# Strassen's scheme for the first feed-forward product of the last two token blocks of a fused attention and two-layer kernel

## The chip, the cores and the metric

The kernel runs on one core of one Trainium2 chip. The metric is the device time of one execution in microseconds (us), smaller is better. The engines of the core are named as in the profile: PE (TensorE, matrix products), PEld (its weight loads, which overlap PE), DVE (VectorE), ACT (ScalarE), POOL (GpSimd) and SP (SyncE, which here only issues DMA transfers).

## The reference

Three stages follow one another. The second and third are what the change touches.

```
x = causal attention with decay (4 batches x 8 heads, 576 positions, 64 wide)   # 2304 tokens x 512
h = x @ w_in                                  # 2304 x 512 @ 512 x 2048
g = maximum(0.01 * h, h)
y = g @ w_out                                 # 2304 x 2048 @ 2048 x 512
h2 = y @ w_in2                                # 2304 x 512 @ 512 x 1024
solu = h2 * softmax(h2)
ln = (solu - mean) / sqrt(var + 1e-6) * g_ln
out = ln @ w_out2                             # 2304 x 1024 @ 1024 x 512
```

All inputs and the output are float32.

## The kernel before

**Numbers.** Every operand of a large product is held as two fp16 halves, a high part and a low part (the rounding rest). One product of a 128x128 piece of weights with a row of tokens is therefore three matmuls: high by high, high by low, low by high. Making the halves takes two instructions for each tile: a copy to fp16 (`copy_f`, any of ACT, DVE, POOL) and a subtraction of that copy from the float32 tile (`sub_f`, DVE or POOL).

**Blocks.** The 2304 tokens are 9 blocks of 256, taken in the order 0, 1, 4, 5, 3, 2, 8, 6, 7. The first feed-forward product of a block is done for 8 pairs of 128-wide pieces of w_in, `k` = 0 to 7, in two groups `g` of four pairs. `hidden` does it for one block and one `k`: 24 matmuls of 256 columns into one PSUM bank `ps_f` (three such banks), then ACT applies leaky relu twice (once into the fp16 tile, once in place), and DVE subtracts the two for the low half. After four `hidden` follows the second product of that block and group, 4 pieces of 24 matmuls of 256 columns.

**Second layer.** `layer2` does a block of the third product (y by w_in2) by Strassen's scheme already: 7 products of 6 matmuls of 512 columns, into banks `ps_g` and halves of the two large PSUM tiles `ph`, with DVE forming the sums out of PSUM (`plus`, `full`). Softmax and normalization follow on ACT, DVE and POOL, then transposes by DMA into `tr`, and the output product, 18 times 24 matmuls of 512 columns. The weights w_in2 and w_out2 are loaded, joined (`whole`), bounded (`bound`, `sums`) and split into halves (`split_w2i`, `load_w2o`, `split_w2o`) ahead of that, beside the feed-forward products.

**Order.** Every instruction is first recorded as an op of a plan, with an engine (or several that may take it), an estimated duration, a priority, the tiles that it reads and writes, and ops that it must follow. A list scheduler in the kernel then turns the plan into one fixed order for each engine; it also gives each op that has several engines to one of them, with the weights `WEIGHT` and `WEIGHT2` on DVE's cost. Tiles belong to tags (`wz`, `y2`, `tr`, `hl2`, `g`, ...) with a fixed number of places; `heirs` passes places that are free for good on to other tags. So a change of priorities, of weights or of tags moves instructions in places far from it. DMA transfers are issued by SP in its own order.

Of the kernel before, what the change touches and what calls it, by code (L numbers as in the profile page):

```python
# [7 lines left out]
F32 = mybir.dt.float32  # L8
# [33 lines left out]
AV = -2.05  # L42
EP = 1307.15
LD = 10.04
# [14 lines left out]
NYO = 2  # L59
NWY = 14  # L60
NY2 = 2
NHL2 = 2
NTR = 3
PWL = 500.0
DMAR = 320.0
YB_ENGS = ("DVE",)
VB_ENGS = ("DVE",)
# [9 lines left out]
US0 = 21.76  # L77
HST = 2.56
TB = 256
# [43 lines left out]
WEIGHT = {"DVE": 7.06}  # L123
WEIGHT2 = {"DVE": 1.06}
HEAT = 0.25
# [280 lines left out]
def body(tc, kqa, kq, vt, f, wa, w2i, w2o, gln, out):  # L406
# [511 lines left out]
    def load_wi(k, prio):  # L918
# [102 lines left out]

    def ffn(blk, g, prio):
        eprio = prio - EP
        first, last = blk not in YO, LEFT.setdefault(blk, 2) == 1
        LEFT[blk] -= 1
# [3 lines left out]
        if first:  # L1029
            YO[blk], YPD[blk] = [P.buf("yo") for q in range(2)], []  # L1030
        gs = {k: hidden(k, XB[blk], prio + HST * i, eprio + i) for i, k in enumerate(GRP[g])}
        for q in range(2):
            ps, yo = P.buf("ps_f"), YO[blk][q]
            for d in range(2):

                def pe(d=d, q=q, ps=ps):
                    for k in GRP[g]:
                        for i in range(2):
                            y_mms(ps.t[:, TB * d:TB * d + TB], 2 * k + i, 2 * q + d, gs[k], k == GRP[g][0] and i == 0, k == GRP[g][-1] and i == 1)

                P.op(PE, 6 * len(GRP[g]) * mmr(TB), pe, prio + YD + 4 * q + 2 * d, r=list(gs.values()) + [WO[2 * k + i] for k in GRP[g] for i in range(2)],
                     **({"w": [ps]} if d == 0 else {"rw": [ps]}))
# [14 lines left out]
    def load_y(blk, prio):  # L1057
        yw, sy, y = P.buf("yw"), P.buf("sy"), P.buf("y2")
        for q in range(2):
# [14 lines left out]
        sub_f(X(2), A(1, 0), X(1), 256, prio, S_ENGS, w=[(sy, 2)], r=[yw, (sy, 1)])  # L1074
        pieces = [(512 * e, 512, lambda e=e: four(yw.t[:, 0:1024])[:, e::2], (yw, "e%d" % e)) for e in range(2)] + [(1024, 768, lambda: four(sy.t), sy)]
        for at, n, v, k in pieces:
            copy_f(lambda at=at, n=n: four(y.t[:, 0, at:at + n]), v, n, prio, scale=lambda: ev(IY + blk), w=[(y, (0, at))], r=[k, (EX, ("iy", blk))])
        for at, n, v, k in pieces:
            sub_f(lambda at=at, n=n: four(y.t[:, 1, at:at + n]), v, lambda at=at, n=n: four(y.t[:, 0, at:at + n]), n, prio, scale=lambda: ev(IY + blk),
                  w=[(y, (1, at))], rw=[k], r=[(y, (0, at)), (EX, ("iy", blk))])  # L1080
        return y

    def layer2(tb, y, prio, oprios):
# [7 lines left out]
        def prod(p, at, n, pr):  # L1091

            def pe():
                for k in range(2):
                    yh, yl = (y.t[:, j, at + 128 * k:at + 128 * k + 128] for j in range(2))
# [5 lines left out]
            P.op(PE, 6 * mmr(512), pe, pr, r=[y, W2I[0, n], W2I[1, n]], w=[p])  # L1101

# [26 lines left out]
    def normal(tt, blk, ps, st, eprio, oprio):  # L1129
# [57 lines left out]
    with tc.manual_schedule():  # L1187
# [44 lines left out]
        P.op(CTL, 1.0, phase2, 0.0, deps=attn_ops)  # L1232
        P.weight = WEIGHT2
# [63 lines left out]
```

## Time and profile before

| | |
|---|---|
| median of 3 runs | 753.83 us (753.05 to 754.22) |
| the profiled execution, own time | 756.95 us |
| its span, first to last instruction | 755.2 us |
| PE busy | 698.0 us, 92% of the span |
| PEld, DVE, ACT, POOL busy | 533.8, 535.7, 502.6, 324.3 us |
| mean granted clock of PE | 0.997 of full speed |

The span is that of the profiled execution alone; its own time is 1.75 us longer than its span, and 3.12 us longer than the median. Attention is over on PE at 410.4 us. What follows, up to the end, is the feed-forward's remainder, the second layer and the output product.

### The profile page before, as it was taken

To read this page: it belongs to the slowest core of one execution; us is meant where nothing else is said; L and a number is where in the kernel's file an instruction comes from. 1 tells how busy PE (TensorE), PEld (TensorE's weight loads), DVE (VectorE), ACT (ScalarE), POOL (GpSimd) and SP (SyncE) were. 2 spreads that over 40 slices of the span, in tenths; PEclk is the share of its full clock that TensorE was granted. 3 is DMA by queue.
4 is the path that set the end of the run, shared out by engine and by line. 5 is a ranking of instruction groups with operands and counts; after the bars stand their busy time and mean duration, and the time that the engine had idled before them with its cause. 6 is when DMAs were issued, how large, how long until landed. Compare 5 with 4: busy or idle time off the path is not lost.

```text
span 755.2 us, 15580 instructions
## 1 busy us (share of the span) xinstructions
PE 698.0 (92%) x5603; PEld 533.8 (71%) x5603; DVE 535.7 (71%) x1420; ACT 502.6 (67%) x1160; POOL 324.3 (43%) x439
## 2 busy tenths in 40 slices
PE   0558789999999999999999999999999999999997
PEld 0346678788788888888889888688866665444443
DVE  5988789878878887777875964351657558788760
ACT  2698999897878789999895666312635435444551
POOL 4466878894365158646522481000422213132220
PEclk9999999999999999999999999999999999999999
DMA  7989489747548766667875414010023242343343
GB/s 214 312 240 230 110 215 232 129 102 158 140 96 164 143 160 128 132 136 148 180 125 142 144 40 154 1 57 1 30 57 84 70 84 81 87 112 70 85 93 102
DMA packets 163902, 94.18 MB, mean 125 GB/s; under 512 B 144224, under 2 KB 144240, under 8 KB 163824
## 3 DMA queue, kind: packets, MB, share of 16 engines
q1 hardware_dynamic: 163792, 93.17, 52.2%
q8 instruction: 44, 0.72, 0.4%
q14 instruction: 34, 0.28, 0.1%
q10 hardware_dynamic: 32, 0.02, 0.0%
HBM read 47.95 MB, written 10.06 MB: 77 GB/s over the span
## 4 chain that ended last, share of the span: by engine, by line
PE 70%; ACT 9%; DVE 5%; DMA 3%; issue 2%; POOL 1%; SPq 0%; ACTq 0%; POOLq 0%; DVEq 0%
PE ps_f L524 47%; PE ps_g L524 8%; PE ps_s L524 6%; PE ph L524 5%; PE ps_v L524 4%; DMA wst<-wa 2%; ACT ps_s L734 2%; ACT hl L478 1%; DVE hl L489 1%; ACT xr L818 1%; ACT kq L478 1%; DVE VT L489 1%; ACT ps_f L1003 1%; DMA pt<-hl 1%; ACT wz L478 1%
## 5 line engine op out<-in xcount | busy, mean ns | idle before, releaser
L524 PEld LDWEIGHTS <-wz 128*128 128x128 f16 x2700 | 262.5, 99 | 39.5 <-issue 5.5
L524 PE MATMUL ps_f<-g,wz 128*128 128x256 f16 x828 | 104.8, 276 | 0.2 <-DVE g L1004 0.2
L489 DVE SCALAR_TENSOR_TENSOR hl<-ps_s,st,hl 128x512 f16<-128x512 f32 (+4 forms) x160 | 82.0, 538 | 17.6 <-ACT hl L478 16.2
L734 ACT ACTIVATE ps_s<-ps_s,st 128x512 f32<-128x512 f32 (+4 forms) x160 | 78.7, 492 | 9.9 <-DVE st L787 8.7
L524 PE MATMUL ps_f<-dec,wz 128*128 128x256 f16 x684 | 84.5, 273 | 0.0
L478 ACT ACTIVATE hl<-ps_s,st 128x512 f16<-128x512 f32 (+4 forms) x157 | 76.6, 524 | 8.9 <-DVE st L755 3.5
L493 POOL TENSOR_TENSOR kq<-raw,kq 64x576 fp32r<-64x576 f32 x64 | 78.2, 1225 | 8.5 <-ACT kq L478 4.1
L524 PEld LDWEIGHTS <-qa 128*128 128x128 f16 x756 | 72.8, 98 | 10.3 <-issue 2.0
L524 PEld LDWEIGHTS <-tr 128*128 128x128 f16 x432 | 42.2, 98 | 49.9
L524 PE MATMUL ps_v<-pt,VT 128*128 128x128 f16 (+1 forms) x928 | 60.3, 216 | 13.2 <-DVE xr L821 9.1
L524 PEld LDWEIGHTS <-y 128*128 128x128 f16 x378 | 36.6, 98 | 45.6 <-issue 3.7
L787 DVE CUSTOM_DVE_ANT_0 ps_s<-ps_s,mask 128x128 f32<-128x128 f32 (+3 forms) x128 | 62.3, 494 | 7.6 <-PE ps_s L524 6.2
L524 PEld LDWEIGHTS <-VT 128*128 128x128 f16 x928 | 53.1, 101 | 20.3 <-issue 9.2
L524 PE MATMUL ps_f<-x,wz 128*128 128x256 f16 x528 | 66.1, 279 | 0.0
L524 PE MATMUL ps_s<-kq 128*128 128x512 f32 (+5 forms) x256 | 60.8, 366 | 1.6 <-DVE hl L489 1.5
L1004 DVE TENSOR_TENSOR g<-ps_f,g 128x512 f16<-128x512 f32 x40 | 27.5, 686 | 26.3 <-ACT ps_f L1003 25.6
L524 PEld LDWEIGHTS ps_s<-kq 128*128 128x128 f32 (+1 forms) x256 | 40.9, 191 | 7.0 <-issue 1.3
L524 PE MATMUL ps_f<-sd,wz 128*128 128x256 f16 x330 | 45.0, 273 | 0.0
L821 DVE SCALAR_TENSOR_TENSOR xr<-ps_v,xr 64x256 f32<-64x256 f32 (+1 forms) x96 | 33.9, 353 | 15.3 <-ACT xr L818 13.9
L1003 ACT ACTIVATE ps_f<-ps_f 128x512 f32<-128x512 f32 x72 | 42.5, 590 | 0.3
L524 PE MATMUL ps_f<-wst,wz 128*128 128x256 f16 x330 | 42.3, 273 | 0.0
L1004 DVE TENSOR_TENSOR dec<-ps_f,dec 128x512 f16<-128x512 f32 x32 | 22.0, 687 | 26.7 <-ACT ps_f L1003 26.5
(252 smaller groups left out, 1382.3 us busy)
## 6 DMA issues: line engine op xcount, KB each, us to landing
wst<-wa SPq DMA_DIRECT2D x32, 512.0 KB
raw<-kq SPq DMA_DIRECT2D x16, 480.0 KB
VT<-vt SPq DMA_DIRECT2D x16, 320.0 KB
raw<-yp_d SPq DMA_DIRECT2D x18, 256.0 KB
raw<-w2i SPq DMA_DIRECT2D x8, 512.0 KB
raw<-w2o SPq DMA_DIRECT2D x8, 512.0 KB
out<-ot SPq DMA_DIRECT2D x16, 256.0 KB
raw<-kqa SPq DMA_DIRECT2D x12, 256.0 KB
```

What stands on the lines that cost most here:

```text
L478: nc.scalar.activation(o, i, CP, scale=1.0 if scale is None else scale)
L489: nc.vector.scalar_tensor_tensor(o, a, scale, b, op0=ALU.mult, op1=ALU.subtract)
L493: (nc.vector if eng == DVE else nc.gpsimd).tensor_tensor(o, a, b, op=op)
L524: nc.tensor.matmul(o, lhsT=l, rhs=r, start=start, stop=stop)
L734: P.op(ACT, act(W, 1, True) + 93, lambda view=view, j=j, k=k: nc.scalar.activation(view(), view(), AF.Exp, bias=sts.t[:, j:j + 1], scale=- ...
L787: P.op(DVE, dve(W) + 130, lambda i=i, j=j, view=view: nc.vector.tensor_tensor_reduce(view(), view(), mask[:, 512 - 128 * i:640], -0.125, 3 ...
L818: P.op(ACT, act(n, 1, True), lambda: nc.scalar.activation(xr.t[a:a + 64, dst0:dst0 + n], ps.t[b:b + 64, c0:c1], CP, scale=PS), prio, w=[(x ...
L821: P.op(DVE, dve(n) + 60, lambda: nc.vector.scalar_tensor_tensor(xr.t[a:a + 64, dst0:dst0 + n], ps.t[a:a + 64, c0:c1], PS, xr.t[a:a + 64, d ...
L1003: P.op(ACT, act(512, 0, True), lambda: nc.scalar.activation(ps.t, ps.t, AF.Prelu, scale=GS, alpha=0.01), eprio, rw=[ps])
L1004: P.op(DVE, dve(512) + 60, lambda: nc.vector.tensor_tensor(g.t[:, 1], ps.t, g.t[:, 0], op=ALU.subtract), eprio, w=[(g, 1)], r=[ps, (g, 0)])
```

## The change

For the last two blocks in the order, 6 and 7, the first product is no longer done block by block. `hidden2` does both blocks at once for one `k`, as a 2x2 block product (two blocks of tokens, two pieces of w_in of the pair, two halves of the 512 inputs) by Strassen's scheme in Winograd's form: 7 products of 6 matmuls in place of 8. The sums of weights are made ahead by `mixed_w`, once for each `k`, the sums of tokens by `mixed_x`, once; each then splits its sums in two fp16 halves. Together they are 96 new instructions: 46 on DVE (29 of 512 elements a row, 17 of 256), 31 on POOL (15, 15 and a copy) and 19 copies on ACT. The sums of the results are 7 DVE additions of 256 elements and one ACT copy for each `k`. PSUM places are one `ps_f` bank for two products, half a bank for a third, and one `ph` tile for the four results. PE's program goes from 3488 to 3440 matmuls of 256 columns, and by as many weight loads; the other matmuls stay. DVE has 1423 in place of 1404 instructions in the order, ACT 991 in place of 936, POOL 540 in place of 444, SP 334 as before.

With it: the joins of w_in2 and w_out2 wait for the last mixing op, the weight on DVE for the second layer's work goes from 1.06 to 2.58, the tag `y2` is parted in two, `wt` is new and hands its places to `y2a`, `tr` and `hl2`, `wz` starts with 3 places of its own in place of 14, `g` has 4 more, and several priorities are others. The scales of two operands and `GS` differ by powers of two.

```diff
-EP = 1307.15
+EP = 1514.57
-NWY = 14
-NY2 = 2
-NHL2 = 2
-NTR = 3
+NWY = 3
+T_HEIRS = ("y2a", "tr", "tr", "hl2", "tr", "tr", "hl2")
+PU = (((6, 7), 1), ((6, 7), 0))
-WEIGHT2 = {"DVE": 1.06}
+WEIGHT2 = {"DVE": 2.58}
...
     def load_w2i(k, h, prio):
         j = 2 * k + h
-        z = ZI[j] = whole(w2i[k, h], prio)
+        z = ZI[j] = whole(w2i[k, h], prio, None, mixed[-1:])
...
     def load_w2o(c, prio):
-        z = ZQ[c] = whole(w2o[c], prio)
+        z = ZQ[c] = whole(w2o[c], prio, None, mixed[-1:])
...
-    def ffn(blk, g, prio):
+    def mixed_w(k, prio, after):
+        za, zb, n, t = P.buf("wz"), P.buf("wz"), P.buf("wz"), P.buf("wt")
+        half = lambda z, h: lambda: z.t[:, 256 * h:256 * h + 256]
+        for z, c in ((za, 2 * k), (zb, 2 * k + 1)):
+            sub_f(lambda z=z: z.t, lambda c=c: W(WI[c], 0), lambda c=c: W(WI[c], 1), 512, prio, M_ENGS, op=ALU.add, w=[z], r=[WI[c]], deps=after)
+        sub_f(half(n, 0), half(zb, 1), half(zb, 0), 256, prio, M_ENGS, w=[(n, 0)], r=[zb])
+        sub_f(half(za, 0), half(zb, 0), half(za, 0), 256, prio, M_ENGS, rw=[(za, 0)], r=[zb])
+        sub_f(half(n, 1), half(zb, 1), half(za, 0), 256, prio, M_ENGS, w=[(n, 1)], r=[zb, (za, 0)])
+        sub_f(half(za, 1), half(za, 1), half(n, 1), 256, prio, M_ENGS, rw=[(za, 1)], r=[(n, 1)])
...
+    def hidden2(k, p, prio, eprio):
+        X, Y, Z, u, ga, gb = P.buf("ps_f"), P.buf("ps_f"), P.buf("ph"), P.buf("hr"), P.buf("g"), P.buf("g")
...
+        P1, P6, P5, C11, C12, C21, C22, r1, u2, u3 = (X, 0), (X, 1), (Y, 0), (Z, 0), (Z, 1), (Z, 2), (Z, 3), (u, 0), (u, 1), (u, 2)
+        for i, (o, xt, xb, w, wb) in enumerate((
+                (P1, old(a11), a11, wold(wa_, 0), wa_), (P6, new(x2), x2, wnew(256), t), (C11, old(a12), a12, wold(wa_, 256), wa_),
+                (C22, new(x3), x3, wnew(0), t), (P5, new(x1), x1, wnew(512), t), (C12, new(x4), x4, wold(wb_, 256), wb_), (C21, old(a22), a22, wnew(768), t))):
...
+            P.op(PE, 6 * mmr(TB), pe, prio + 0.2 * i, w=[o] + ([(ga, "slot"), (gb, "slot")] if i == 0 else []), r=[xb, wb])
+        P.op(ACT, act(256, 0, True), lambda: nc.scalar.activation(at(r1)(), at(P1)(), CP), eprio, w=[r1], r=[P1])
...
+        plus(u2, P6, r1, w=[u2], r=[P6, r1])
+        plus(C11, C11, r1, rw=[C11], r=[r1])
+        plus(u3, C22, u2, w=[u3], r=[C22, u2])
+        plus(C22, P5, u3, rw=[C22], r=[P5, u3])
+        plus(u2, P5, u2, rw=[u2], r=[P5])
+        plus(C12, C12, u2, rw=[C12], r=[u2])
+        plus(C21, C21, u3, rw=[C21], r=[u3])
...
+        for i, (do, x, pr) in enumerate(steps):
+            do(x, pr, mixed[i - 2:i - 1] if i > 1 else opened)
+            mixed.append(P.ops[-1])
```

Three places in the orders follow. On PE, after the last `hidden` of a single block, the program before goes over to the first product of the second layer (operand `y20`, weights `wy9`, `wy2`, `wy12`); each line stands for the matmuls and weight loads of its kind that follow it.

```order
L524 MATMUL ps_f0_166<-wst0_98,qa_112 128x256
...
L524 LDWEIGHTS y20_5569
L524 MATMUL ps_g0_5554<-wy9_5564,y20_5569 128x512
...
L524 MATMUL ps_g0_5554<-wy2_5557,y20_5569 128x512
...
L524 MATMUL ph0_5552<-wy12_5567,y20_5569 128x512
```

In the changed program the first Strassen group stands at that place (tokens `sd0`, `sd1`, `wst0`, `x0`, `x1`, `x2`, `wz15`, weights `qa` and mixed weights `wt0`); each of these rows stands six times.

```order
L532 MATMUL ps_f2_168<-wst0_98,wz16_79 128x256
...
L532 MATMUL ps_f0_166<-sd0_93,qa_112 128x256
...
L532 MATMUL ps_f0_166<-sd1_94,wt0_5541 128x256
...
L532 MATMUL ph0_5532<-wst0_98,qa_112 128x256
...
L532 MATMUL ph0_5532<-x2_109,wt0_5541 128x256
...
L532 MATMUL ps_f1_167<-x0_107,wt0_5541 128x256
...
L532 MATMUL ph0_5532<-wz15_78,qa_112 128x256
...
L532 MATMUL ph0_5532<-x1_108,wt0_5541 128x256
...
L532 MATMUL ps_f2_168<-sd2_95,qa_112 128x256
```

The second layer's first product stands 498 matmuls of 256 columns later than this group's start; the bank `ps_f2` is needed again right behind the group.

On DVE, around the same place, the program before subtracts the last single blocks' halves (L1004), joins the weights of the second layer (L896), and starts the sums of the second layer (L1108, L1104).

```order
L1004 TENSOR_TENSOR g3_106<-ps_f2_168,g3_106 128x512
L896 SCALAR_TENSOR_TENSOR wy0_5555<-raw1_91,wk1_97 128x512
L1004 TENSOR_TENSOR dec1_102<-ps_f2_168,dec1_102 128x512
L1004 TENSOR_TENSOR dec0_101<-ps_f0_166,dec0_101 128x512
L1108 ISA ph0_5552,s20_5580<-ph0_5552,wst1_99 128x512
L1108 ISA s20_5580 128x1
L1104 TENSOR_TENSOR sd2_95<-ps_g0_5554,wst1_99 128x512
```

In the changed program the last mixing of `wt7` (L501) stands right ahead, and the additions of the first group (L1093) between joins (L904).

```order
L501 TENSOR_TENSOR wt7_5548<-qa_112,wt7_5548 128x512
L904 SCALAR_TENSOR_TENSOR wy1_5536<-raw0_90,wk0_96 128x512
L1012 TENSOR_TENSOR g0_103<-ps_f2_168,g0_103 128x512
L1093 TENSOR_TENSOR hr0_5553<-ps_f0_166,hr0_5553 128x256
L1093 TENSOR_TENSOR ph0_5532<-ph0_5532,hr0_5553 128x256
L1093 TENSOR_TENSOR hr0_5553<-ph0_5532,hr0_5553 128x256
L904 SCALAR_TENSOR_TENSOR wz7_70<-raw1_91,wk1_97 128x512
L1093 TENSOR_TENSOR ph0_5532<-ps_f1_167,hr0_5553 128x256
L1093 TENSOR_TENSOR hr0_5553<-ps_f1_167,hr0_5553 128x256
L1093 TENSOR_TENSOR ph0_5532<-ph0_5532,hr0_5553 128x256 x2
L1107 TENSOR_TENSOR g2_105<-ph0_5532,g2_105 128x512
L1107 TENSOR_TENSOR g1_104<-ph0_5532,g1_104 128x512
```

So the joins of the second layer's weights moved behind the mixing, and the group's eight results come out in one row of DVE instructions.

On POOL, before the first output product, the program before splits two chunks of w_out2 (`wy8` and `x2` by L492 and L493) and then goes over to the normalization's small steps (`s20`).

```order
L492 TENSOR_SCALAR wy8_5563<-wy8_5563,ex_116 128x512
L493 TENSOR_TENSOR wy7_5562<-wy8_5563,wy7_5562 128x512
L492 TENSOR_SCALAR x2_109<-x2_109,ex_116 128x512
L493 TENSOR_TENSOR wy3_5558<-x2_109,wy3_5558 128x512
L1147 TENSOR_SCALAR s20_5580<-s20_5580 128x1
L1148 TENSOR_TENSOR s20_5580<-s20_5580,halfm_114 128x1
```

In the changed program POOL also has the low halves of normalized rows (`wt4`, `wt5`, 1024 elements) and of y (`y2b0`, `y2a0`), all ahead of one of the last chunks (`x1`).

```order
L500 TENSOR_SCALAR sy0_5556<-sy0_5556,ex_116 128x768
L501 TENSOR_TENSOR y2b0_5539<-sy0_5556,y2b0_5539 128x768
L501 TENSOR_TENSOR wt4_5545<-raw1_91,wt4_5545 128x1024
L501 TENSOR_TENSOR wt5_5546<-raw0_90,wt5_5546 128x1024
L500 TENSOR_SCALAR raw2_92<-raw2_92,ex_116 128x4x128
L501 TENSOR_TENSOR y2a0_5538<-raw2_92,y2a0_5538 128x512
L500 TENSOR_SCALAR sd0_93<-sd0_93,ex_116 128x512
L501 TENSOR_TENSOR x1_108<-sd0_93,x1_108 128x512
```

The 18 subtractions of 1024 elements, which stood on DVE, moved to POOL, and the chunk `x1` stands behind four of them.

## Rows read from the trace of the kernel before

**Rows 1.** The page's first row.

```profile
span 755.2 us, 15580 instructions
```

**Rows 2.** Busy time of each engine in six stretches from 412 us to 752 us.

```profile
core 0: us, PE busy (x) PEld busy (x) DVE busy (x) ACT busy (x) POOL busy (x), PEclk, DMA share, GB/s
...
412.00:476.00 64.00, 64.00 (x590) 57.44 (x588) 41.35 (x79) 39.14 (x77) 28.55 (x28) 1.00 0.29 100
476.00:531.00 55.00, 54.79 (x463) 44.95 (x461) 20.07 (x46) 13.97 (x25) 1.42 (x2) 1.00 0.06 20
531.00:611.00 80.00, 80.00 (x561) 54.63 (x559) 53.32 (x112) 40.86 (x68) 25.06 (x41) 1.00 0.24 59
611.00:700.00 89.00, 88.70 (x461) 44.98 (x460) 66.10 (x156) 39.08 (x56) 21.38 (x39) 1.00 0.38 91
700.00:752.00 52.00, 50.18 (x231) 22.32 (x229) 27.25 (x56) 22.56 (x33) 9.53 (x22) 1.00 0.44 97
```

**Rows 3.** Timeline of all engines at the end: start, duration, engine, instruction.

```profile
750.56 0.81 PE L524 MATMUL ps_g<-wz,tr 128*128 128x512 f16 x3
751.46 0.69 ACT L1178 ACTIVATE ot<-ps_g,ex 128x512 f32<-128x512 f32 x1 [4.49 <-PE ps_g L524]
752.17 0.33 SPq L515 DMA_DIRECT2D out<-ot  x1
```

**Rows 4.** Timeline of PE, runs of equal matmuls, from attention's end on.

```profile
410.36 2.78 PE L524 MATMUL ps_f<-wst,wz 128*128 128x256 f16 x24
...
431.56 2.78 PE L524 MATMUL ps_f<-wst,wz 128*128 128x256 f16 x24
434.18 2.78 PE L524 MATMUL ps_f<-wst,qa 128*128 128x256 f16 x24
...
478.80 1.46 PE L524 MATMUL ps_g<-wy,y 128*128 128x512 f16 x6
480.09 1.24 PE L524 MATMUL ph<-wy,y 128*128 128x512 f16 x5
```

**Rows 5.** Waits of PE from 400 us on: line, releaser, total, times, longest.

```profile
PE ph L524 <- DVE sd L1104: 1.4, 2, 1.2
```

**Rows 6.** Groups of DVE by line and shape: count, busy us, mean ns, idle before.

```profile
L493 DVE TENSOR_TENSOR hl<-raw,hl 128x1024 f16<-128x1024 f32 x18 | 22.8, 1282 | 6.7 <-ACT hl L478 6.6
...
L1104 DVE TENSOR_TENSOR sd<-ph,sd 128x512 f32<-128x512 f32 x9 | 6.2, 690 | 4.3 <-PE ph L524 4.1
...
L493 DVE TENSOR_TENSOR sy<-raw 128x256 f32<-128x256 f32 x8 | 3.6, 450 | 1.2 <-POOL x L493 1.2
...
L493 DVE TENSOR_TENSOR wy<-wy,sd 128x512 f32<-128x512 f32 x1 | 0.7, 677 | 0.0
```

**Rows 7.** Groups of POOL by line and shape, the same columns.

```profile
L493 POOL TENSOR_TENSOR wz<-wz,wz 128x512 f16<-128x512 f32 x19 | 24.1, 1267 | 1.6
...
L492 POOL TENSOR_SCALAR wz<-wz,ex 128x512 f32<-128x512 f32 x25 | 18.7, 748 | 4.3 <-ACT qa L478 2.6 <-ACT wy L478 1.5
L493 POOL TENSOR_TENSOR x<-xr,x 128x256 f16<-128x256 f32 x16 | 11.4, 713 | 24.3 <-ACT x L478 23.8
L1148 POOL TENSOR_TENSOR s<-s,halfm 128x1 f32<-128x1 f32 x18 | 11.3, 626 | 1.5
```

**Rows 8.** Timeline of DVE and POOL, 442 us to 449 us.

```profile
442.65 1.20 POOL L493 TENSOR_TENSOR wst<-wy,wst 128x512 f16<-128x512 f32 x1
...
445.98 1.47 POOL L493 TENSOR_TENSOR wy<-wy,wy 128x512 f16<-128x512 f32 x1
446.36 1.64 DVE L489 SCALAR_TENSOR_TENSOR wy<-wz,ex,wy 128x512 f16<-128x512 f32 x1
...
448.52 0.74 DVE L489 SCALAR_TENSOR_TENSOR sd<-wy,ex,sd 128x512 f16<-128x512 f32 x1
```

More of the change, by code (lines that the diff above doesn't have):

```diff
@@ L59 @@
 NYO = 2
-NWY = 14
-NY2 = 2
-NHL2 = 2
-NTR = 3
+NWY = 3
+T_HEIRS = ("y2a", "tr", "tr", "hl2", "tr", "tr", "hl2")
 PWL = 500.0
 DMAR = 320.0
-YB_ENGS = ("DVE",)
+YB_ENGS = ("DVE", "ACT")
 VB_ENGS = ("DVE",)
@@ L77 @@
 US0 = 21.76
-HST = 2.56
+HST = 2.72
 TB = 256
@@ L139 @@
 S_ENGS = ("DVE", "POOL")
+M_ENGS = ("DVE", "POOL")
+MH_ENGS = ("ACT", "DVE", "POOL")
 N_ENGS = ("DVE", "ACT")
@@ new lines, in mixed_x @@
+    def mixed_x(p, prio, after):
+        (a11, a12), (a21, a22) = XB[p[0]], XB[p[1]]
+        z11, z12, z21, n = (P.buf("wz") for _ in range(4))
+        x = lambda a, j: lambda: a.t[:, j]
+        v = lambda z: lambda: z.t
+        for z, a in ((z11, a11), (z21, a21), (z12, a12)):
+            sub_f(v(z), x(a, 0), x(a, 1), 512, prio, M_ENGS, op=ALU.add, w=[z], r=[a], deps=after)
+        sub_f(v(n), v(z11), v(z21), 512, prio, M_ENGS, w=[n], r=[z11, z21])
+        for j in range(2):
+            sub_f(v(z21), v(z21), x(a22, j), 512, prio, M_ENGS, op=ALU.add, rw=[z21], r=[a22])
+        sub_f(v(z11), v(z21), v(z11), 512, prio, M_ENGS, rw=[z11], r=[z21])
+        sub_f(v(z12), v(z12), v(z11), 512, prio, M_ENGS, rw=[z12], r=[z11])
+        out = []
+        for z in (z21, z11, n, z12):
+            t = P.buf("wz")
+            copy_f(lambda t=t: as_g(t.t)[:, 0], v(z), 512, prio, engs=MH_ENGS, w=[(t, 0)], r=[z])
+            sub_f(lambda t=t: as_g(t.t)[:, 1], v(z), lambda t=t: as_g(t.t)[:, 0], 512, prio, M_ENGS, w=[(t, 1)], r=[z, (t, 0)])
+            out.append(t)
+        SX[p] = out
@@ new lines, in ffn @@
+    def ffn(blks, g, prio):
+        eprio = prio - EP
+        if len(blks) == 1:
+            gs = [{k: hidden(k, XB[blks[0]], prio + HST * i, eprio + i) for i, k in enumerate(GRP[g])}]
+        else:
+            both = {k: hidden2(k, blks, prio + HS2 * i, eprio + i) for i, k in enumerate(GRP[g])}
+            gs = [{k: x[e] for k, x in both.items()} for e in range(2)]
+        for blk, gk, at in zip(blks, gs, (YD,) if len(blks) == 1 else PYS):
+            ffn_out(blk, g, gk, prio + at, eprio, 4 if len(blks) == 1 else QS)
@@ L1091, in prod @@
         def prod(p, at, n, pr):
+            yy, at = y[at // 1024], at % 1024
             def pe():
                 for k in range(2):
-                    yh, yl = (y.t[:, j, at + 128 * k:at + 128 * k + 128] for j in range(2))
+                    yh, yl = (yy.t[:, j, at + 128 * k:at + 128 * k + 128] for j in range(2))
                     wh, wl = (W(W2I[k, n], j) for j in range(2))
@@ L1213, in body @@
         nc.sync.dma_start(glt, gln)
-        for n, (blk, g) in enumerate(UN + tuple((blk, g) for blk in ORDER for g in range(2) if (blk, g) not in UN)):
-            ffn(blk, g, 1000.0 + US0 * n)
         def phase2():
@@ L1223, in phase2 @@
             P.tag("wz", tiles(bp, "wy", NWY, [128, 512], F32))
-            P.tag("y2", tiles(bp, "y2", NY2, [128, 2, 1792], F16))
+            P.tag("y2a", tiles(bp, "y2a", 1, [128, 2, 1024], F16))
+            P.tag("y2b", tiles(bp, "y2b", 2, [128, 2, 768], F16))
+            P.tag("wt", tiles(bp, "wt", NG, [128, 1024], F32))
+            P.tag("g", tiles(bp, "g", 4, [128, 2, 512], F16))
+            P.tag("hr", tiles(bp, "hr", 2, [128, 768], F32))
             wide.append(bp.tile([128, DF2], BF16, name="wide"))
             P.tag("sy", tiles(bp, "sy", 1, [128, 768], F32))
-            P.tag("hl2", tiles(bp, "hl2", NHL2, [128, 2048], F16))
-            P.tag("tr", tiles(bp, "tr", NTR, [128, 16, 128], F16))
             P.tag("ot", tiles(bp, "ot", 2, [128, 512], F32))
             P.tag("s2", tiles(bp, "s2", 4, [128, 21], F32))
-        P.op(CTL, 1.0, phase2, 0.0, deps=attn_ops)
+        opened = [P.op(CTL, 1.0, phase2, 0.0, deps=attn_ops)]
+        paired = {(x, g) for p, g in PU for x in p}
+        n = 0
+        pairs = list(dict.fromkeys(p for p, g in PU))
+        P.weight = WEIGHT2
+        steps = [(mixed_w, k, WTP[i] + j) for i, g in enumerate(dict.fromkeys(g for p, g in PU)) for j, k in enumerate(GRP[g])]
+        for i, p in zip((MX, len(steps) + 1), pairs):
+            steps.insert(i, (mixed_x, p, XSP + i))
+        for i, (do, x, pr) in enumerate(steps):
+            do(x, pr, mixed[i - 2:i - 1] if i > 1 else opened)
+            mixed.append(P.ops[-1])
+        P.weight = WEIGHT
+        for blks, g in [((x,), g) for x, g in UN] + [((x,), g) for x in ORDER for g in range(2) if (x, g) not in UN and (x, g) not in paired] + list(PU):
+            ffn(blks, g, 1000.0 + US0 * n + (PUS if len(blks) > 1 else 0.0))
+            n += len(blks)
         P.weight = WEIGHT2
```

78 lines of the change are left out of this document (58 added, 20 removed).

## The prediction

> **What bounds the kernel now.** I read the busy time by stretches first, because the change touches only what follows attention. From 412 to 700 us PE is busy for 287.5 of 288 us, and 50.2 of the last 52; the granted clock is 1.00 in every stretch, the upper of PE's two levels (2.4 GHz) [rows 2]. Then the waits: from 400 us on PE waits for an instruction for 1.4 us in all, twice, for DVE's sums of the second layer [rows 5]. Last the end: PE issues its last matmuls at 750.56 us, ACT copies the last tile at 751.46, and the store is issued at 752.17 [rows 3]. So PE alone sets the time after attention, with under 2 us lost from 412 us to its end and a tail of some 4 us, from PE's end to the end of the span at 755.2 [rows 1], which the change doesn't touch. A matmul that is taken out of PE's program should come out of the time whole, provided that nothing takes PE's place as the bound.
>
> **What a matmul costs there.** Two runs of 24 matmuls of 256 columns start at 431.56 and 434.18: 2.62 us, 0.109 us for each. From 410.36 to the second layer's first product at 478.80 PE has 624 of them (and four small ones): 68.44 us, 0.110 for each. Six of 512 columns take from 478.80 to 480.09, 0.215 each [rows 4]. Weight loads overlap: PEld is busy 57.44 us beside PE's 64.00 [rows 2], so the 48 loads removed are no term of their own.
>
> **The change, part by part.**
>
> *Removed from PE:* 8 groups of 48 matmuls become 8 of 42, so 48 x 0.109 = 5.24 us. Up to attention's end the work of PE is the same, and nothing is added on PE.
>
> *Handovers in the Strassen groups.* In a group the seven results go into two `ps_f` banks and one `ph` tile, and DVE's seven additions (0.45 us for 256 elements, 3.2 us) and two subtractions of 512 (1.4 us) and ACT's five short passes follow [rows 6]. That is about 4.6 us of DVE for 4.6 us of PE (42 x 0.109), where a single block's group has 0.69 us of DVE for 2.62. Does PE wait for the banks? The groups don't stand close: by PE's own counting of matmuls from 410.36 they begin at about 476, 483, 496, 503, 508, 513, 528 and 547 us, with second products between them, and at 490 to 530 DVE is lightly used in the program before (20.07 of 55 us from 476 to 531) [rows 2]. The closest are the third to sixth, four groups in 17 us, in which `ph` comes round every second group, so after about 9 us. No row of before shows this handover itself. The nearest is that of the second layer's blocks, which form the same sums from the same sort of banks: nine blocks cost PE 1.4 us, 0.16 each [rows 5]. Bounds for eight groups: nothing (second products lie between), and 8 x 0.16 = 1.24 us. I take the middle, 0.6 us.
>
> *Mixing, 96 instructions.* On DVE 29 x 0.677 + 17 x 0.450 = 27.3 us; on POOL 15 x 1.267 + 15 x 0.713 + 0.75 = 30.5 us [rows 6, 7]; 19 copies on ACT, at POOL's 0.75 for a scaling of that size some 14 us. They lie between attention's end at 410 and the first Strassen group, 600 matmuls later, at about 476. What stood there before, the joins, bounds and splits of the second layer's weights (most of DVE's 41.35, ACT's 39.14 and POOL's 28.55 us [rows 2]), is moved behind them. By my count of the new order with these prices DVE has 41 us in this stretch, POOL 39: 64 us are there for them. PE doesn't wait for the mixing except at the groups, and the first needs only `mixed_w` of its own `k`, which stands first in the chain, and `mixed_x`. I cost it at nothing; the cover is the 600 matmuls. If DVE comes out of this stretch late, the first that PE misses is the `ps_f2` bank, right behind the first group, 4.6 us on: some 3 to 4 us of lateness are free.
>
> *Moved second-layer weights.* Joins and splits of w_in2 go into 476 to 531, where DVE had 20.07, ACT 13.97 and POOL 1.42 of 55 us, and of w_out2 into 531 to 611, with 53.32, 40.86 and 25.06 of 80 [rows 2]. The second layer's first product also moves, from 478.80 to about 531 us by counting, and the first output product to about 610. So there is room on each engine, and the need comes later too. Cost nothing; SP has as many instructions as before, and the DMA share was 0.06 and 0.24 in these stretches, so later loads find the queues free.
>
> *DVE to POOL.* The 18 subtractions of 1024 elements leave DVE (18 x 1.282 = 22.8 us) [rows 6] and cost POOL about twice its 512 price, 2.5 us each, 46 us. From 531 on POOL was busy 56 of 221 us [rows 2]; with them it is near 100, DVE is relieved. Each of them stands in the chain from normalization to transposes to output product, longer by 1.3 us, but PE has other work: the order puts a block's output products behind the next blocks' products. Lower bound nothing, upper bound the 1.4 us of DVE's waits again; I take nothing.
>
> *The waits of before.* DVE's late sum at 704 us cost PE most of the 1.4 us [rows 5]. With fewer long instructions on DVE it may vanish. Between 1.4 us gained and none, I count none, since another POOL step may come in its place.
>
> **Sum.** 756.95 - 5.24 + 0.6 = 752.3 us on the profiled execution's own time. That execution lies 3.12 us above the median of the runs shown, 753.83, so on the median it is 753.83 - 4.64 = **749.2 us**. A difference of 0.2%, 1.5 us, is about the least that a measurement of this kernel can tell from none.
>
> **The rivals.**
>
> A. *The Strassen groups wait for their sums.* Each group's results pass ACT, then a chain of DVE additions in order, with joins and subtractions of other work between them on DVE. One wait of 1.17 us, such as before has once at the longest [rows 5], in each group makes 9.4 us: 749.2 - 0.6 + 9.4 = 758.0. The gain is used up from 5.24 / 8 = 0.65 us in each group on; slower by more than 0.2% it is from (5.24 + 1.5) / 8 = 0.84. For it: 4.6 us of DVE for 4.6 of PE in a group, and a place where `ph` is reused 9 us on. Against it: second products of 2.62 us a piece between most groups, and little else on DVE there. Weaker versions end between 750 and 753. 0.14.
>
> B. *DVE and POOL get in each other's way while mixing.* At 446 us a DVE instruction of 512 elements with two operands in SBUF took 1.64 us while a POOL subtraction took 1.47; beside other neighbours the same forms took 0.74 and 1.20 [rows 8]. If they took strict turns, DVE's 26 us of such instructions and POOL's 38.5 would need 64.5 us of the 64, and with DVE's 9 to 10 us of other work up to 74: DVE 10 us late, of which 3 to 4 are free, so up to 6 or 7 us lost: 749.2 + 6.5 = 755.7, no gain once it is over 4.6. Against it: in most of this stretch DVE and POOL overlapped before at about their usual durations, and 28.55 us of POOL beside 41.35 of DVE in 64 kept PE at 64.00 [rows 2]. 0.07.
>
> The Trainium skill, page "SBUF — State Buffer", section "Who interferes with whom", says that a DVE instruction with two SBUF inputs and a GpSimd one that reads SBUF exclude each other for whole instructions; by that rule B's lateness would be the larger one, and the rows at 446 us agree with it, the stretch as a whole only in part.
>
> C. *POOL late with w_out2.* From about 568 us, when the last bound of w_out2 is known, POOL has in order some 9 subtractions of 512 (11.4 us), 10 scalings (7.5), 3 of 256 (2.2), a pair of 768 (2.8), four of 1024 (10) and four rounds of four small steps of 0.626 or less (6 to 10): 40 to 44 us, with no waits counted, so `x1` is split at 608 to 612. The first output product begins at about 610 and comes to `x1` after 18 matmuls, at 614 [rows 4, 7]. The margin is 2 to 6 us; if POOL's work takes 23% longer, as its 1.47 against 1.20 did [rows 8], or waits as long, that is 10 us, and PE loses 4 to 8 once: 749.2 + 4 to 8 = 753 to 757, no gain from 4.6 on. Against it: POOL may start some of this earlier than I put it, and PE's own small waits shift the deadline. 0.08.
>
> D. *More is gained.* The 1.4 us of waits goes with DVE's relief, and the groups cost nothing: 749.2 - 0.6 - 1.4 = 747.2, or 746.9 if the smaller holes go as well (0.3 us from 611 to 700 [rows 2]). 0.05.
>
> **How the numbers follow.** The forecast has 0.66, with its own range of 747.0 to 751.5: the waits of before gone at the one end, and at the other a handover of 2.9 us in place of 0.6. With A 0.14, C 0.08, B 0.07 and D 0.05, some 0.14 of A to C lie above 754.5 and a few hundredths below 746.5, so the range is 746.5 to 754.5. Faster by over 0.2% means below 752.3: the forecast, D, and a fifth of A to C (weak versions): 0.66 + 0.05 + 0.06 = 0.77. Between 752.3 and 755.3: 0.11, the middle of A to C. Above: 0.12, A first.
>
> **What the changed profile would show.** PE busy near 693 us, the 256-column matmuls 48 fewer, and from 412 us on PE at 99% in every stretch; PE's last matmul near 746 in a span near 750.5. The first Strassen group should begin at 476 within 1 us, the second layer's first product near 531, the first output product near 610. DVE 41 us and POOL 39 in 412 to 476, and PE 64.0. If A is right, waits of `ps_f` or `ph` on L1093 or L1107 stand at the top of PE's waits between 476 and 560; if B, DVE additions there take over 1 us each and PE waits at 476 or 481; if C, PE waits for a POOL split between 610 and 620, or for `tr`. The forecast is wrong if PE's idle time from 412 on grows by more than 3 us at any of these places, or if the granted clock of a stretch falls below 1.00 behind such a wait.

## The result and the profile after

The changed kernel takes 759.47 us (median; 757.75 to 760.08), the kernel before 753.44 us (751.77 to 754.22) on the same chip. The ratio is 1.0074 with an interval of 1.0047 to 1.0102: slower. The forecast was 749.2 us. The profiled execution of the changed kernel has an own time of 760.08 us and a span of 758.3 us.

The busy time of the changed kernel by stretches, with the columns of [rows 2]:

```profile
412.00:476.00 64.00, 64.00 (x589) 57.39 (x587) 50.57 (x72) 32.35 (x63) 42.64 (x40) 1.00 0.05 18
476.00:531.00 55.00, 52.82 (x475) 46.13 (x474) 38.57 (x93) 34.88 (x70) 21.86 (x23) 1.00 0.33 115
531.00:611.00 80.00, 75.81 (x508) 50.30 (x506) 58.72 (x138) 59.67 (x97) 53.85 (x70) 0.98 0.29 77
611.00:700.00 89.00, 87.99 (x422) 40.99 (x420) 49.97 (x129) 53.21 (x79) 55.26 (x72) 1.00 0.47 110
```

The mixing stretch, 412 to 476 us, costs PE nothing: 64.00 of 64. The holes lie where the eight Strassen groups stand: PE is idle for 2.18 us from 476 to 531 and for 4.19 us from 531 to 611, where [rows 2] have 0.21 and 0.00. PE's waits from 405 us on, total, times and longest, name the place:

```profile
PE ph L532 <- DVE hr L1093: 2.8, 4, 1.5
PE ph L532 <- DVE ph L1093: 1.7, 4, 0.5
PE ph L532 <- DVE s L1206: 1.5, 4, 0.6
PE ph L532 <- DVE ex L691: 0.5, 1, 0.5
```

L1093 are the additions of the groups; in the kernel before, [rows 5] was all there is. The wait on `ex` (another DVE instruction, which ended last by the profile) stands at the same place inside a group, between two of its products, so nine waits in five of the groups take 5.0 us. The first group in the timeline (start, length, engine, instruction, idle time before and its releaser):

```profile
475.83 0.82 PE L532 MATMUL ph<-wst,qa 128*128 128x256 f16 x6
...
476.45 0.43 DVE L1093 TENSOR_TENSOR hr<-ps_f,hr 128x256 f32<-128x256 f32 x1
476.49 0.82 PE L532 MATMUL ph<-x,wt 128*128 128x256 f16 x6
...
477.14 0.82 PE L532 MATMUL ps_f<-x,wt 128*128 128x256 f16 x6
...
477.34 0.43 DVE L1093 TENSOR_TENSOR ph<-ph,hr 128x256 f32<-128x256 f32 x1 [0.47 <-PE ph L532]
477.81 0.42 DVE L1093 TENSOR_TENSOR hr<-ph,hr 128x256 f32<-128x256 f32 x1
...
478.29 0.72 PE L532 MATMUL ph<-wz,qa 128*128 128x256 f16 x5 [0.33 <-DVE hr L1093]
```

The reader is to see who waits for whom. The result tile `ph` holds two PSUM banks: C11 and C12 go into one, C21 and C22 into the other. The product C11 (first product row) is done at about 476.65, and DVE is free from 476.88, when its addition on `ps_f` ends. Yet DVE's addition on C11 starts only at 477.34, behind the end of C22 (second product row) at 477.31. PE's next product on the tile, C12, waits until DVE's second addition, which reads C22 in the other bank, ends at 478.23. So PE and DVE take turns on the tile.

A wait costs PE more than its idle time. Without one a product starts 0.65 us after the one before it (477.14 after 476.49), though its row lasts 0.82; with one PE runs empty first. From these rows I estimate 0.17 us more for each wait: 6.5 us for the nine waits in the groups.

The cost is read best from attention's end to the last product's end, which leaves attention's own scatter out. Before: 410.36 to 750.56 + 0.81 [rows 3, 4], 341.01 us. After:

```profile
408.87 2.78 PE L532 MATMUL ps_f<-wst,wz 128*128 128x256 f16 x24
...
753.71 0.81 PE L532 MATMUL ps_f<-wz,wt 128*128 128x512 f16 x3
```

This makes 345.65 us, 4.64 more than before, where 48 matmuls fewer should make 335.77. So 9.9 us were lost behind attention: by that estimate 6.5 in the groups, some 1.7 in other waits beyond those of before (2.2 us in seven in place of 1.4 in two), and 1.6 by a lower clock, which the last section shows.

### The profile page after: what moved, and what is told of

Same layout as the page of the kernel before. It is cut to its first block, busy times and chain, and to the rows that moved or that the text cites. A ratio compares the mean times of both kernels' runs of the same rounds, so it can differ in the third digit from the quotient of the medians.

```text
span 758.3 us, 15708 instructions
## 1 busy us (share of the span) xinstructions
PE 696.3 (92%) x5555; PEld 529.8 (70%) x5555; DVE 537.6 (71%) x1439; ACT 544.7 (72%) x1229; POOL 427.7 (56%) x535
## 4 chain that ended last, share of the span: by engine, by line
PE 63%; ACT 12%; DVE 12%; DMA 5%; issue 4%; POOL 4%; SPq 0%; ACTq 0%; POOLq 0%; DVEq 0%
PE ps_f L532 43%; PE ph L532 6%; PE ps_s L532 6%; PE ps_g L532 5%; PE ps_v L532 4%; ACT ps_s L742 2%; ACT hl L486 2%; DMA pt<-hl 2%; DVE hl L497 2%; DMA wst<-wa 2%; DMA raw<-kqa 1%; DVE ph L1093 1%; ACT wk L486 1%; ACT xr L826 1%; DVE VT L497 1%
## 5 line engine op out<-in xcount | busy, mean ns | idle before, releaser
L532 PEld LDWEIGHTS <-wz 128*128 128x128 f16 x2532 | 246.5, 99 | 41.3 <-issue 8.6
L532 PE MATMUL ps_f<-g,wz 128*128 128x256 f16 x948 | 119.5, 276 | 0.2 <-DVE g L1012 0.2
L532 PEld LDWEIGHTS <-wt 128*128 128x128 f16 x720 | 70.2, 98 | 67.6 <-issue 4.5
L501 POOL TENSOR_TENSOR kq<-raw,kq 64x576 fp32r<-64x576 f32 x64 | 78.6, 1232 | 8.2 <-ACT kq L486 3.0
L532 PE MATMUL ps_f<-dec,wz 128*128 128x256 f16 x564 | 71.7, 274 | 0.0
L501 POOL TENSOR_TENSOR wt<-raw,wt 128x1024 f16<-128x1024 f32 (+1 forms) x23 | 44.8, 1957 | 12.0 <-ACT wt L486 11.4
L532 PE MATMUL ps_f<-x,wz 128*128 128x256 f16 x396 | 50.9, 280 | 0.0
L826 ACT ACTIVATE xr<-ps_v 64x256 f32<-64x256 f32 (+1 forms) x96 | 31.1, 324 | 15.6 <-PE ps_v L532 10.7
L532 PE MATMUL ps_f<-wz,wt 128*128 128x512 f16 x162 | 41.5, 379 | 0.0
L532 PE MATMUL ps_s<-qa 66*128 66x128 f32 (+1 forms) x32 | 12.1, 553 | 29.1 <-DMA qa<-sd 18.9
L532 PE MATMUL ps_f<-x,wt 128*128 128x512 f16 (+1 forms) x165 | 38.2, 348 | 0.0
```

The source lines that it names most:

```text
L501: (nc.vector if eng == DVE else nc.gpsimd).tensor_tensor(o, a, b, op=op)
L532: nc.tensor.matmul(o, lhsT=l, rhs=r, start=start, stop=stop)
L826: P.op(ACT, act(n, 1, True), lambda: nc.scalar.activation(xr.t[a:a + 64, dst0:dst0 + n], ps.t[b:b + 64, c0:c1], CP, scale=PS), prio, w=[(x ...
```

## The experiments

The column "PE stretch" is that time, worked out in the same way from the one profiled execution of each; ratios are to the kernel before, run beside it. In e9_blind 48 matmuls more stand ahead of attention's end, so 5.24 us are added to its 340.44. Kernels were run on several chips, on which the kernel before took 755.08 to 756.04 us, so a range that an expectation gives in us belongs to 753.44 us, and is compared by the ratio.

| kernel | ratio (interval) | PE stretch, us |
|---|---|---|
| changed kernel | 1.0074 (1.0047 to 1.0102) | 345.65 |
| e1_order | 1.0006 (0.9987 to 1.0024) | 341.97 |
| e2_aside | 0.9967 (0.9948 to 0.9986) | 339.96 |
| e3_plain | 1.0162 (1.0137 to 1.0187) | 353.99 |
| e4_bank | 1.0176 (1.0151 to 1.0201) | 356.49 |
| e5_tile | 1.0008 (0.9987 to 1.0030) | 341.76 |
| e7_two | 0.9998 (0.9973 to 1.0023) | 341.84 |
| e8_plan4 | 0.9939 (0.9920 to 0.9958) | 336.98 |
| e8_plan2 | 1.0006 (0.9990 to 1.0023) | 342.36 |
| e8_plan3 | 0.9968 (0.9950 to 0.9986) | 339.55 |
| e9_blind | 1.0057 (1.0036 to 1.0078) | 345.68 |
| r_plan4 | 0.9925 (0.9909 to 0.9941) | 337.02 |
| r_after | 1.0044 (1.0026 to 1.0063) | 344.04 |

**e2_aside: the additions off the result tile.**

```diff
+        aside = lambda q: at((u, 0) if q[0] is Z else q)()
         def plus(o, a, b, **kw):
-            P.op(DVE, dve(256) + 60, lambda: nc.vector.tensor_tensor(at(o)(), at(a)(), at(b)(), op=ALU.add), eprio, **kw)
+            P.op(DVE, dve(256) + 60, lambda: nc.vector.tensor_tensor(aside(o), aside(a), aside(b), op=ALU.add), eprio, **kw)
```

> The order of every engine is that of the changed kernel. The DVE additions of the Strassen groups read and write a spare part of an SBUF tile wherever they touched the result tile in PSUM, so the sums are left out of the result; the number, size and place of the additions stay. Theory 1 (bank): without DVE in the banks PE writes on, the waits inside the groups go, 752 to 753.5 us. Theory 2 (chain of additions on a busy DVE): about half of it stays since the two passes of ACT and the subtractions still wait in DVE's queue, 755 to 757. Theory 3 (mixing, the shared port, moved work): 758 to 761.

Measured: 0.9967, 752.42 us. Against 753.44 that is 751.0, an us under theory 1's range and far from the others. With the order of every engine the same and as many additions on DVE, 5.7 us of the stretch go (345.65 to 339.96; 4.1 beside the changed kernel's second profile, r_after). No wait for an addition is left; the largest that remain are of the kind of [rows 5] and the handover of `ph` from one group to the next:

```profile
PE ph L532 <- DVE s L1208: 1.4, 5, 0.4
PE ph L532 <- DVE g L1109: 1.0, 1, 1.0
PE ps_g L532 <- DVE va L672: 0.7, 1, 0.7
```

Theory 3, that mixing or moved work takes the time, falls; theory 2 as well, unless most of it is in the tile. The kernel leaves the sums out of the result, and its additions no longer wait for the products either; so e2 prices the place, and doesn't say which of the two waits matters.

**e1_order: the two products of a bank side by side.**

```diff
-                (C22, new(x3), x3, wnew(0), t), (P5, new(x1), x1, wnew(512), t), (C12, new(x4), x4, wold(wb_, 256), wb_), (C21, old(a22), a22, wnew(768), t))):
+                (C12, new(x4), x4, wold(wb_, 256), wb_), (C22, new(x3), x3, wnew(0), t), (C21, old(a22), a22, wnew(768), t), (P5, new(x1), x1, wnew(512), t))):
```

> The seven products of a Strassen group are issued in another order, so that the two products of each PSUM bank of the result tile follow each other (C11, C12, then C22, C21, then P5); nothing else in the source is changed. Theory 1 (bank): in the changed kernel PE's sixth and seventh product wait because DVE still adds in the other half of their bank; these waits are 5.4 us, and 1.6 us more go to the lower clock after the longest one. With both products of a bank ahead of the additions they go: 751 to 754 us against 759.5. Theory 2 (chain): PE waits because DVE's chain of additions is long and stands between other work; the chain then only moves, and the time stays at 758 to 761. Theory 3 (mixing and moved work take the time): no change, 758 to 761.

Measured: 1.0006, 755.36 us. Against 753.44 that is 753.9, at the upper end of theory 1's range, but the trace doesn't show what theory 1 said; waits on the additions stay, in seven groups:

```profile
PE ph L532 <- DVE ph L1093: 4.5, 7, 1.3
```

The first group there:

```profile
475.17 0.82 PE L532 MATMUL ph<-wz,qa 128*128 128x256 f16 x6
475.83 0.82 PE L532 MATMUL ph<-x,wt 128*128 128x256 f16 x6
476.69 0.43 DVE L1093 TENSOR_TENSOR ph<-ph,hr 128x256 f32<-128x256 f32 x1 [1.12 <-PE ph L532]
477.17 0.38 PE L532 MATMUL ph<-x,wt 128*128 128x256 f16 x2 [0.52 <-DVE ph L1093]
```

C11's bank is complete with C12 (first row) at 475.99, yet its addition starts at 476.69, when C22 in the other bank has ended, and C21, also in the other bank, waits 0.52 us for that addition. So my theory 1 was too narrow. Theory 4: the program's waits treat the two-bank tile as one, whichever bank is touched. That it is the program's waits is read from the releasers, which the profile infers from semaphore events. The kernel's plan keeps the four quarters apart and sees none of this.

The Trainium skill, page "PSUM — Partial Sum Buffer", section "PSUM bank collisions raise a hardware error", says that two engines must not be in the same bank at once. That asks for waits within a bank; the rows above show them across banks too, which that rule doesn't ask for.

**e7_two: only the two additions between the products off the tile**, which are the one on C11 and the one that reads C22.

```diff
-        plus(C11, C11, r1, rw=[C11], r=[r1])
-        plus(u3, C22, u2, w=[u3], r=[C22, u2])
+        plus(C11, C11, r1, True, rw=[C11], r=[r1])
+        plus(u3, C22, u2, True, w=[u3], r=[C22, u2])
```

> The order is that of the changed kernel. Of the seven additions of a group only two touch a spare SBUF tile in place of the result tile: the one on C11 and the one that reads C22, which stand between the products of the tile; the sums are thereby wrong in the result, and the five later ones act on PSUM as before. Theory 4: the waits in the groups are made by these two alone, so the time falls nearly as far as with all seven aside (ratio 0.997): 0.996 to 0.9995. Theory 2 (a long chain on DVE): the chain has the same length and place, ratio 1.004 to 1.008.

Measured: 0.9998, just above what theory 4 gave and clear of theory 2's range. The length and place of DVE's chain is as before, and two additions of seven bring back most of it (0.0076 of e2's 0.0107 in the ratio; 2.2 of 4.1 us beside r_after). What is left of the waits in groups is 2.6 us, where a later addition comes ahead of C21:

```profile
PE ph L532 <- DVE ph L1093: 2.6, 3, 1.7
```

**e5_tile: the rule told to the plan**, on top of e1: the first additions on the tile follow all four of its products.

```diff
-            P.op(PE, 6 * mmr(TB), pe, prio + 0.2 * i, w=[o] + ([(ga, "slot"), (gb, "slot")] if i == 0 else []), r=[xb, wb])
+            P.op(PE, 6 * mmr(TB), pe, prio + 0.2 * i, w=[o, (o[0], "all")] + ([(ga, "slot"), (gb, "slot")] if i == 0 else []), r=[xb, wb])
-        plus(C11, C11, r1, rw=[C11], r=[r1])
-        plus(u3, C22, u2, w=[u3], r=[C22, u2])
+        plus(C11, C11, r1, rw=[C11], r=[r1, (Z, "all")])
+        plus(u3, C22, u2, w=[u3], r=[C22, u2, (Z, "all")])
```

> The products of a group stand as in e1 (C11, C12, C22, C21, P5), and the plan is told that the first additions on the two-bank result tile come after all four products that write it. Theory 4 (whole tile, formed after e1: an addition on one bank of the tile and a product on its other bank also wait for each other): the 4.5 us of waits of e1 go, 752 us or a little less beside 753.4 (ratio 0.995 to 1.000), unless the plan's new order costs something later. Theory 1 (only the same bank waits): e1's waits were something else and stay, ratio 1.000 to 1.003.

Measured: 1.0008, so no gain: by the time alone theory 1's range, not theory 4's. But the waits that theory 1 said would stay are gone, as theory 4 said: none on L1093 is left. Others stand in their place, in the order that the plan made anew:

```profile
PE ph L532 <- DVE g L1107: 1.7, 3, 1.1
PE ps_g L532 <- ACT wst L1216: 1.5, 1, 1.5
PE ph L532 <- DVE raw L1237: 1.4, 1, 1.4
```

**e8_plan4, e8_plan2, e8_plan3: e5 with other numbers of the plan.** The edit of the first:

```diff
-PUS = -15.0
+PUS = -20.95
-WEIGHT2 = {"DVE": 2.58}
+WEIGHT2 = {"DVE": 2.78}
```

> e5 with two numbers of the plan changed (when the paired groups begin, and the weight on DVE for the second layer's work), at which the plan sees no wait of PE at all behind attention. Theory 4 (the waits on the two-bank tile were the main loss, and e5 lost its gain to the order that the plan chose): PE needs 337 to 340 us from attention's end to its last product, against 341.0 before and 341.8 in e5; ratio 0.992 to 0.998. Theory 5 (what is left is the handover of the result tile between groups and of sums that DVE makes late, since its mixing takes longer beside POOL than the plan reckons): 340 to 342 us and a ratio of 0.998 to 1.002.

> e5 with four numbers of the plan changed (when a pair's second products begin, one output priority, and a higher weight on DVE), again with no wait of PE in the plan. Theory 4: 337 to 340 us from attention's end, ratio 0.992 to 0.998. Theory 5: 340 to 342 us, ratio 0.998 to 1.002; with more work on POOL, waits for its splits.

> e5 with five numbers of the plan changed (the groups begin 9 units earlier, second products follow their group sooner, DVE's weight a little lower), again with no wait of PE in the plan. Theory 4: 337 to 340 us, ratio 0.992 to 0.998. Theory 5: 340 to 342 us, ratio 0.998 to 1.002; the groups begin earlier, so the mixing may be late for the first of them.

Measured: 0.9939, 1.0006 and 0.9968; the first and the third lie in theory 4's range, the second in theory 5's. The first needs 336.98 us for PE's stretch, 1.2 above the 335.77 that the count of matmuls gives. All its waits from 403 us on:

```profile
PE ph L532 <- DVE raw L1237: 0.9, 1, 0.9
PE ps_f L532 <- ACT hr L1090: 0.5, 1, 0.5
PE ph L532 <- DVE s L1206: 0.5, 3, 0.2
PE ps_g L532 <- DVE va L672: 0.2, 1, 0.2
```

The second shows that the rule alone isn't enough. It met theory 5: PE waits for the tile to come free of the group before.

```profile
PE ph L532 <- DVE g L1107: 3.9, 5, 1.4
```

**e9_blind: a plan without waits, but without the rule.** The changed kernel with one number (`YD` 20.39 in place of 18.14).

> The changed kernel with its own order of products and without the rule on the tile; one number of the plan is changed (when a single block's second product begins), so that its plan too sees no wait of PE behind attention. Theory 4 (the plan doesn't see the waits on the two-bank tile): they stay, 4 to 6 us in the groups, 343 to 346 us from attention's end to the last product, ratio 1.003 to 1.008. Theory 6 (the gain of the best version came from a plan without waits, not from the rule): 337 to 340 us, ratio 0.993 to 0.998.

Measured: 1.0057, 345.68 us, as theory 4 gave; theory 6 falls. By its own reckoning its plan is as free of waits as that of e8_plan4, and on the chip the groups wait for 6.4 us:

```profile
PE ph L532 <- DVE ph L1093: 3.5, 5, 1.4
PE ph L532 <- DVE hr L1093: 2.9, 5, 1.3
```

One thing stays open: e8_plan4 has e1's order of products besides the rule, and e9 neither. No run has e1's order with such a plan and without the rule.

**r_plan4 and r_after: the best version and the changed kernel on one chip.**

> The same kernel as e8_plan4 again, beside the changed kernel on one chip. Theory 4: ratio 0.992 to 0.996 to the kernel before, over 1% under the changed kernel. If the earlier result was chance: 0.997 to 1.001.

> The changed kernel again, beside the best version on one chip. Every theory: ratio 1.005 to 1.010 to the kernel before, with waits of 4 to 6 us inside the groups in its trace.

Measured: 0.9925 (0.9909 to 0.9941; 750.14 us) and 1.0044 (1.0026 to 1.0063; 758.07 us) beside 755.52 us of the kernel before. The best version is 7.9 us faster than the changed kernel, and faster than the kernel before. r_after came out a little under the range expected of it.

**Two whose times don't decide.** e3_plain takes the 48 matmuls back and drops the additions (first line below), e4_bank delays additions until both products of their bank are done (the others, for one addition):

```diff
+        for i, (o, w, off, xs) in enumerate(((C11, wa_, 0, (a11, a12)), (C12, wb_, 0, (a11, a12)), (C21, wa_, 0, (a21, a22)), (C22, wb_, 0, (a21, a22)))):
...
-        plus(C11, C11, r1, rw=[C11], r=[r1])
+        plus(C11, C11, r1, rw=[(Z, "b0"), C11], r=[r1])
```

> The mixing, the moved work, the weights and priorities stay as in the changed kernel, and the groups of two blocks stay, but the products are 8 plain ones of 6 matmuls accumulated in PSUM (48 more matmuls, no additions, the mixed operands are made and not used). Theory 1 and 2: 5.2 us of matmuls come back and the waits on additions go; what is left is the price of mixing and moved work, 1 to 2 us over the kernel before: 754 to 756. Theory 3: the waits stay and the matmuls come back: 762 to 765.

> The products keep the order of the changed kernel; the plan is told that an addition on a bank must follow both products of that bank, so the additions start later and stand in DVE's order behind them. Theory 1 (bank): no product waits for an addition of its own group; the additions end about 1.5 us later in each group: 751 to 755. Theory 2 (chain): the chain is later by 1 to 2 us in each of eight groups, 762 to 770. Theory 3: 758 to 761.

Measured: 1.0162 and 1.0176, against 753.44 us 765.6 and 766.7. The first lies just above theory 3's range, the second in theory 2's, but e4's trace has no wait on an addition. In both the plan made another order, with other waits; the first of these rows is the largest of e3, the other two are the largest of e4:

```profile
PE ph L532 <- ACT ph L1092: 5.3, 4, 1.8
```

```profile
PE ps_f L532 <- POOL wt L501: 4.2, 1, 4.2
PE ps_g L532 <- DVE y2b L497: 4.0, 1, 4.0
```

The row of e3 is worth a look, since this kernel has no sums at all. Here a third product of twelve matmuls (C21) goes into the second bank, while ACT's two passes on the first bank are due:

```profile
502.63 1.47 PE L532 MATMUL ph<-x,wz 128*128 128x256 f16 x12
...
504.14 0.60 ACT L1091 ACTIVATE g<-ph 128x512 f16<-128x512 f32 x1 [1.30 <-PE ph L532]
...
505.26 0.63 ACT L1092 ACTIVATE ph<-ph 128x512 f32<-128x512 f32 x1
...
505.94 1.47 PE L532 MATMUL ph<-x,wz 128*128 128x256 f16 x12 [1.78 <-ACT ph L1092]
```

ACT's first pass starts when C21 has ended, and C22, in the second bank as well, waits 1.78 us until ACT is done in the first. Such waits stand in seven groups of e3, 7.3 us in all. That is theory 4 again, with another engine and without an addition. So e3's time is no clean price of the mixing, and not theory 3 either; e4 shows only that a different order can cost more than the waits that it removes.

## Why the prediction was wrong

**The step that failed is "Handovers in the Strassen groups", taken at 0.6 us.** I transferred 0.16 us a block from the second layer's sums, and let DVE's additions run beside PE's products. The runs showed that on the result tile they take turns: the groups wait for 5.0 us in place of 0.6, by my estimate 6.5 with PE running empty. e2, without additions on the tile, is 5.7 us faster in the stretch than the first profile of the changed kernel and 4.1 us faster than the second, r_after (344.04 to 339.96). The difference of the two profiles, 1.6 us, is the clock's, which fell behind the longest wait of the groups in the one and not in the other.

The nearest row was near in kind and not in proportion. A product of the second layer takes 1.29 us [rows 4] and an addition 0.69 [rows 6]; in the groups a product takes 0.65 us and an addition 0.43, and little work of PE's stands between. That longer products hide the turns in the second layer is argued, no run shows it. I looked for the handover from group to group (when `ph` comes round) and didn't look at the tile inside a group.

**Removed matmuls: right.** PE's own work fell as counted. In r_plan4 the stretch is 337.02 us, 3.99 less than before, with five waits of 2.0 us where before has two of 1.4. Its ratio of 0.9925 is about the 0.9939 that 749.2 to 753.83 makes, but that is a chosen plan, the best of three, and no proof of the forecast's sum.

**Mixing hidden: right for PE, wrong in size on DVE.** I counted 41 us on DVE and 39 on POOL from 412 to 476; they are 50.57 and 42.64, and PE still has 64.00, since there was room in the 64 us.

**Moved weights: right.** PE doesn't wait for a split of w_in2 or w_out2 in the changed kernel.

**The other waits:** I had counted no net change. The changed kernel has 2.2 us of waits outside the groups' products where [rows 5] had 1.4, and e2, where the groups don't hold PE up, has 4.5. This is the second, smaller error: 1.7 us by the estimate above in the changed kernel, some 3 us in e2.

**The profiled execution.** The sum was made against 756.95 us and carried over with 3.12 us of difference to the median. The changed kernel's profiled execution lies only 0.61 above its median, so of the 10.3 us between forecast and median 7.8 us are the sum's and 2.5 that transfer's. The range's lower end of 747.0 was also put down to the waits of before alone, which make 749.2 - 1.4 = 747.8.

**The rivals.** A named the right place, waits inside the groups on L1093. Its reason, a DVE busy with joins, wasn't the cause, by e2 and e7. That its 758.0 us came near the measured 759.47 was luck: it had 9.4 us of waits in the groups, where some 6.5 were lost, and the rest came from the clock, other waits and the transfer to the median. B's premise was right in part, DVE was later by 9.6 us than I counted, and cost PE nothing. C doesn't show in the changed kernel, but its kind does in e4, at 629 us. D's ratio, 747.2 to 753.83 or 0.9912, is just under r_plan4's 0.9925 and inside its interval; but 2.0 us of waits are left there, where D had none.

## What to carry to other kernels

Before a scheme that forms sums in PSUM is costed, look at who touches the same tile between its products. Where two engines take turns on a tile, as here with products of 0.65 us and additions of 0.43, no count of either engine's work shows it. A plan that keeps finer parts of a tile apart than the program's waits do will put instructions where they stall, so tell it the coarser rule, and then look for the order again. A price taken from another place needs the same ratio of product to sum, not only the same form.

## What the runs showed of the hardware

Beside POOL, DVE's mixing instructions with two operands in SBUF took up to 2.6 times the 677 ns of [rows 6]; in the changed kernel from 408 to 476 us:

```profile
L501 DVE TENSOR_TENSOR wt<-qa,wt 128x512 f16<-128x512 f32 x3 | 3.5, 1176 | 0.0
L501 DVE TENSOR_TENSOR wy<-wz 128x512 f32<-128x512 f16 x2 | 2.8, 1392 | 0.0
L501 DVE TENSOR_TENSOR x<-wz,x 128x512 f16<-128x512 f32 x1 | 1.8, 1752 | 0.0
```

Of the 29 mixing instructions of 512 elements in DVE's timeline, 15 took 0.97 to 1.75 us, and each of these overlaps with an instruction of POOL; 14 took 0.68 or 0.69, and 11 of these overlap with none. What the 15 took beyond 0.68 adds up to 9.5 us, about all of the 9.6 by which DVE's 50.57 us exceed my 41. The rule of the Trainium skill that rival B cites (page "SBUF — State Buffer", section "Who interferes with whom") agrees in kind.

The clock fell in one execution and not in another with the same waits. Two stretches of the changed kernel around its longest wait, and the same in r_after:

```profile
532.00:536.00 4.00, 2.46 (x17) 1.49 (x16) 2.58 (x5) 2.83 (x6) 3.25 (x5) 1.00 0.00 0
536.00:540.00 4.00, 3.48 (x19) 2.37 (x18) 3.08 (x6) 2.82 (x5) 3.41 (x4) 0.59 0.03 6
```

```profile
532.00:536.00 4.00, 2.26 (x14) 1.16 (x12) 2.23 (x6) 2.60 (x6) 3.63 (x5) 1.00 0.00 0
536.00:540.00 4.00, 3.68 (x32) 3.13 (x32) 3.60 (x6) 3.61 (x7) 3.46 (x4) 1.00 0.03 6
```

Waits of 1.54 and 0.52 us stand there in both. The second row is at 0.59 in the one, so partly at the lower of PE's two levels (1.2 GHz), with 19 matmuls in place of 32, and at 1.00, 2.4 GHz, in the other. What that cost is read from the product behind the second wait to the second layer's product `y2b`, first in the changed kernel, then in r_after:

```profile
536.83 1.44 PE L532 MATMUL ph<-x,wt 128*128 128x256 f16 x6 [0.52 <-DVE ph L1093]
...
541.72 0.81 PE L532 MATMUL ps_g<-qa,y2b 128*128 128x512 f16 x3
```

```profile
536.32 0.82 PE L532 MATMUL ph<-x,wt 128*128 128x256 f16 x6 [0.52 <-DVE ph L1093]
...
539.60 0.81 PE L532 MATMUL ps_g<-qa,y2b 128*128 128x512 f16 x3
```

The same matmuls take 4.89 us in the one and 3.28 in the other, 1.61 more, and that is the whole difference of the two stretches (345.65 and 344.04).
